# The h product in 64x64 waves, a slot of two 64x64 runs and two full-array phases, and PSUM as one pair plus three rotating pairs

## The chip, the cores and the metric

The kernel runs on one core of a Trainium2 chip. The metric is device time in microseconds, the median over repeated runs of the whole kernel; a profile is one further execution, taken by the hardware profiler, and its times are microseconds from the start of its span. The engines are PE (TensorE, matrix products, with PEld for its weight loads), DVE (VectorE), ACT (ScalarE), POOL (GpSimd) and SP (SyncE, which issues transfers). Each engine works through its own instructions in order and waits on semaphores for the others. PE writes its results to PSUM, eight banks of 512 fp32 values per partition; ACT and DVE read them from there.

## The reference

Four batches of eight heads run a state recurrence over 768 tokens with head size 40; its output, 3072 tokens by 320, goes through a two-layer block with a softmax weighting and a layer norm:

```python
for t in range(S):                       # S = 768, state is (B, H, 40, 40)
    y[:, :, t] = einsum('bhd,bhde->bhe', r[t], state)
    Sa = einsum('bhde,bhe->bhd', state, a[t])
    state = state * w[t][:, :, None, :] - outer(Sa, b[t]) + outer(v[t], k[t])
x = y.transpose(0, 2, 1, 3).reshape(3072, 320)
h = x @ w_in                             # 3072 x 1024
e = exp(h - max(h)); solu = h * e / (sum(e) + 1e-9)
ln = (solu - mean(solu)) / sqrt(var(solu) + 1e-6) * g_ln
out = ln @ w_out                         # 3072 x 320
```

The two weights arrive as fp64 and are converted to fp32 on the chip from their bits.

## The kernel before

The recurrence is done in chunks of 64 tokens. An item `i` (there are `N` = 24) is one chunk of two batches: 2 x 64 tokens, eight heads each, in 128 partitions. Two sequences of items alternate (even and odd `i`), so the state that item `i` leaves is next used by item `i + 2`. A hand-written order fixes every engine's instructions (`manual_schedule`): the main loop runs over slots `i` = -1 to 27, and in each slot works on several items at different stages:

- item `j = i + 5`: `front` and `front_b` transpose the raw `a` and the scaled `b` on PE (tiles `pa`, `pb`); DVE multiplies `pa` by the decays `ex` into `aT` (L374), ACT copies `pb` to `bT` (L359). `norm` multiplies them (`pnt`), DVE masks the result to `nt` (L383), and it goes through DRAM to `invert`, a triangular inverse done in 30 steps on DVE (L436, L438), of which `some(n)` issues `n` at a time. `decay` and `decay_turned` prepare the decays of items `j + 2` and `j + 1`: a product `pcum`, two exponentials on ACT, a transpose `pei`, and an ACT copy to `ex` (L366).
- item `i + 2`: `attend_kv` and `attend_r` transpose k, v and r (`pk`, `pv`, `pr`) and ACT copies each (L359).
- item `i + 1`: `scores` (`ps`, masked twice by DVE), `couple` (`py`) and `close` (`pz`), which finish the inverse, `carried` and `driven` (`px`).
- item `i`: `solved` (`pu`), `stated` (transposes of the state, `pst`, copied by ACT to `s`), `answered` (`pl`), `read` in two parts (`pyo`), and `leave`, in which DVE forms the output rows and the new state and SP and POOL (`left`, one slot later) move the rows to `xT` by DMA.
- item `i - 3`: `hidden`, the product `h = xT . w_in` of 128 x 1024 with a contraction of 320 that is cut into parts 128, 128 and 64; then `highest` (DVE, L678), `exped` (ACT), `weighed` and `spreadof` (DVE), and `folded` (eight transposes `plnT` in two halves, each copied by ACT to `lnT`, L721).
- item `i - 4`: `output`, `po = lnT . w2`, 8 products of 128x128x320, scaled by ACT to `osb` (L735), which issues the DMA to the output itself.

PE's products come in two shapes of the array. The recurrence's products use it as four tiles of 64x64 (16 products of up to 104 columns each per step; `in_turn` deals them out so that four neighbours lie in four different tiles). The transposes, `pcum`, `po` and the parts 0 and 1 of `h` use it whole; part 2 of `h` uses two tiles of 64 rows by 128 columns, because its contraction is 64. `fence()` is a PE drain; it stands once in every slot, ahead of the second half of `read`.

PSUM is divided by tag: `banks` (two buffers of two banks, for the 64x64 products), `h` (one buffer of two banks) and `bank` (two buffers of one bank, for transposes, `pcum`, `po`, `pmean`). A tile is free for its tag's next user when all its readers are done.

The order of PE in a slot far from the ends is: `pu`, `ps`, `pst`, `pa`, h(0,1), `pb`, `pei`, h(1,1), `pcum`, first half of `po`, `py`, `pnt`, `pl`, second half of `po`, `pz`, first half of `pyo`, `px`, h part 2, drain, second half of `pyo`, `px`, `plnT`, h(0,0), `pk`, `pv`, h(1,0), `pr`. The h of one item spans two slots.

Of the kernel before, what the change touches and what calls it, by code (L numbers as in the profile page):

```python
# [17 lines left out]
P = 128  # L18
# [6 lines left out]
LAG = 1  # L25


THIN = (5, 15)
# [23 lines left out]
def kernel(  # L52
# [34 lines left out]
    ps1 = ctx.enter_context(tc.tile_pool(name="ps1", bufs=2, space=PSUM))  # L87
    ps2 = ctx.enter_context(tc.tile_pool(name="ps2", bufs=1, space=PSUM))
    ps3 = ctx.enter_context(tc.tile_pool(name="ps3", bufs=2, space=PSUM))
# [49 lines left out]
    def banks(name):  # L139
        return ps1.tile([P, 2, 512], FP32, tag="banks", name=name)  # L140

    def bank(name):
        return ps3.tile([P, 512], FP32, tag="bank", name=name)
# [76 lines left out]
    def turn_g():  # L220
        pg = bank("pg")
        nc.tensor.transpose(out=pg[:, 0:NF], in_=g_rows, identity=ident[0:NF, 0:NF])
        for x, y in zip(g_cols, (0, -20, -36)):
            nc.scalar.mul(out=x, in_=pg[:, 0:NF], mul=2.0 ** y)
# [6 lines left out]
    def mean_of(lo, hi, begun):  # L231
        t = bank("pmean")
        nc.tensor.matmul(t[:, 0:DM], lhsT=ident, rhs=begun, start=True, stop=False)
        mean_part(t, lo, hi, False)
        return mean_kept(t)
# [90 lines left out]
    def decay(i):  # L326
        if not ok(i):
            return
        d = st[i]
        if "lw" not in d:  # L330
            logged(i)
        t = (bank("pcum") if i > 5 else ps2.tile([P, DFF], FP32, tag="h", name="h"))[:, 0:DM]
        nc.tensor.matmul(t, lhsT=c_("cum"), rhs=d["lw"], start=True, stop=True)  # L333
        nc.scalar.activation(out=ei_t[0][:, :, 0:D], in_=heads(t), func=AF.Exp)
        inv = d["inv"] = two.tile([P, DM], FP32, tag="inv", name="inv", bufs=4)
        nc.scalar.activation(out=inv, in_=t, func=AF.Exp, scale=-1.0)
# [10 lines left out]
    def turned(name, x):  # L347
        t = bank("p" + name)
        for j in range(4):
            nc.tensor.transpose(out=t[0:W2, j * P:(j + 1) * P],  # L350
                                in_=x[:, 2 * j:2 * j + 2].rearrange("p a b -> p (a b)")[:, 0:W2], identity=ident)
        return t[0:W2].rearrange("p (j b t) -> p b j t", j=4, b=2)
# [9 lines left out]
    def decay_turned(i):  # L362
        if not ok(i):
            return
        ex = st[i]["ex"] = ex_t[i % (AHEAD + 2)]
        nc.scalar.copy(out=ex[0:W2, :, :, 1:], in_=turned("ei", ei_t[0]))  # L366

    def front(i):
        if not ok(i):
            return  # L370
        d = st[i]
        t = turned("a", d["raw_a"])
        aT = d["aT"] = tokens("aT", AHEAD)
        nc.vector.tensor_tensor(out=aT[0:W2], in0=t, in1=d["ex"][0:W2, :, :, 0:C], op=ALU.mult)  # L374

    def front_b(i):
        if not ok(i):
            return
        d = st[i]
        d["bT"] = kept("bT", turned("b", d["kb"][:, H:]))  # L380
# [13 lines left out]
    def norm(i):  # L394
        if not ok(i):
            return
        d = st[i]
        t = banks("pnt")
        for u in in_turn(lambda p, q, g, h: (h, p ^ h)):
            p, q, g, h = u  # L400
            j = 2 * q + g
            mm(t[half(p ^ h), h, j * C:j * C + C], keyed(d["bT"], u), keyed(d["aT"], u))
        nt = d["nt"] = tokens("nt", AHEAD)
        masked(nt, t[:, :, 0:256])
        n, at = divmod(i, GRP)
        if at == 0:
            blocks[n] = dram.tile([2 * GRP * H, C, C], FP32, tag="nt_dram", name="nt_dram")
        queue = nc.sync if i < 4 else nc.gpsimd
        queue.dma_start(out=blocks[n].rearrange("(a h x) s c -> a x s h c", a=GRP, x=2)[at].rearrange("x s h c -> (x s) h c"),  # L409
                          in_=nt.rearrange("p h j c -> p (h j) c"))  # L410
# [56 lines left out]
    def couple(i):  # L467
        if not ok(i):
            return
        d = st[i]  # L470
        t = banks("py")
        for u in in_turn(lambda p, q, g, h: (p ^ h, p)):
            p, q, g, h = u
            j = 2 * q + g
            x = half(p ^ h)
            mm(t[half(p), h, j * Q:j * Q + Q], d["nt"][x, h, j], d["tu"][x, 4 * h + j, 0:Q])
        nc.scalar.activation(out=wy[:, :, :, 0:Q], in_=t[:, :, 0:4 * Q].rearrange("p h (j c) -> p h j c", j=4),  # L477
                             func=AF.Copy, scale=c_("neg_hi"))

    def close(i):  # L480
        if not ok(i):
            return
        d = st[i]
        t = banks("pz")
        for u in in_turn(lambda p, q, g, h: (p, p ^ h)):
            p, q, g, h = u
            j = 2 * q + g
            mm(t[half(p ^ h), h, j * Q:j * Q + Q], wy[half(p), h, j], d["uh"][half(p), 2 * (4 * h + j) + (p ^ h)])
        nc.scalar.copy(out=d["tu"].rearrange("p (h j) c -> p h j c", h=2)[:, :, :, 2 * Q:],
                       in_=t[:, :, 0:4 * Q].rearrange("p h (j c) -> p h j c", j=4))  # L490


    def attend_kv(i):
        if not ok(i):
            return
        d = st[i]
        d["kT"] = kept("kT", turned("k", d["kb"]))
        d["vT"] = kept("vT", turned("v", v_t[0]))

    def attend_r(i):  # L500
        if not ok(i):
            return
        st[i]["rT"] = kept("rT", turned("r", r_t[0]), 2)

    def stated(i):
# [4 lines left out]
        if ci:  # L510
            t = bank("pst")
# [6 lines left out]
    def scores(i):  # L518
# [3 lines left out]
        t = banks("ps")  # L522
# [13 lines left out]
    def carried(i):  # L536
# [5 lines left out]
        d["px"] = banks("px")  # L542
# [21 lines left out]
    def solved(i):  # L564
# [3 lines left out]
        t = banks("pu")  # L568
# [14 lines left out]
    def answered(i):  # L583
# [3 lines left out]
        t = banks("pl")  # L587
# [6 lines left out]
    def read(i, own):  # L594
# [4 lines left out]
        if own:  # L599
            d["po"] = banks("pyo")  # L600
# [60 lines left out]
    def hidden(i, some):  # L661
# [4 lines left out]
        for kt, x in some:  # L666
            if (kt, x) == (NK - 1, 0):
                d["h"] = ps2.tile([P, DFF], FP32, tag="h", name="h")
            part = slice(0, P) if kt < 2 else half(x)
            mm(d["h"][:, 512 * x:512 * x + 512], d["xT"][part, kt], w_in[part, 2 * kt + (x if kt < 2 else 0)],  # L670
               start=kt == NK - 1, stop=kt == NK - 2)
# [39 lines left out]
    def folded(i):  # L711
# [3 lines left out]
        lnT = d["lnT"] = two.tile([P, NF, P], FP32, tag="lnT", name="lnT", bufs=1)  # L715
        for x in range(2):
            t = bank("plnT")
# [5 lines left out]
    def output(i, x):  # L723
# [4 lines left out]
        if x == 0:  # L728
            d["out"] = bank("po")
        for f in range(x * NF // 2, x * NF // 2 + NF // 2):  # L730
            nc.tensor.matmul(d["out"][:, 0:DM], lhsT=d["lnT"][:, f, :], rhs=w2[:, f, :], start=f == 0, stop=f == NF - 1)  # L731
        if x == 0:
            return
        osb = two.tile([P, DM], FP32, tag="osb", name="osb", bufs=1)
        nc.scalar.activation(out=osb, in_=d["out"][:, 0:DM], func=AF.Copy, scale=d["rs"])  # L735
# [28 lines left out]
    decay(0)  # L764
    logged(1)
    decay_turned(0)
    for i in range(4):
# [6 lines left out]
        front_b(i)  # L774
        decay(i + 1)
# [3 lines left out]
        norm(i)  # L779
        decay_turned(i + 1)  # L780
# [28 lines left out]
    scores(0)  # L809
    decay(5)  # L810
# [12 lines left out]
    for i in range(-1, N + 3 + LAG):  # L823
        j, m = i + AHEAD, i - LAG
        pieces = shares.get(i, (0, 5, 4, 4) if i % GRP else (3, 5, 4, 5))
# [8 lines left out]
        if i in THIN:  # L834
            stated(i)
            front(j)
        if i >= 0:
            scores(i + 1)
        if i >= 0:
            load_keys(j + 3, "w")  # L840
        load_keys(j + 2, "bak")

        if i not in THIN:
            stated(i)
            front(j)
        hidden(m - 2, ((0, 1),))
        if i == 3 + LAG:
            centred(mean)
        narrow(some_weights[1], pieces[1])
        front_b(j)  # L850
        if ok(j + 2):
            logged(j + 2)
        if i == 1 + LAG:
            first = ps2.tile([P, DFF], FP32, tag="h", name="mean")
            mean_part(first, 0, 2, True, False)
        decay_turned(j + 1)
        hidden(m - 2, ((1, 1),))
        flip(i + 1)
        highest(m - 2)
        scaled(j + 1)  # L860
        left(i - 1)
        if i == 1 + LAG:
            mean_part(first, 2, 3, False)
            mean = mean_kept(first)
        decay(j + 2)
        output(m - 3, 0)

        some(pieces[2])
        if i == 2 + LAG:
            mean = mean_of(3, 6, mean)  # L870
        couple(i + 1)
        exped(m - 2)
        norm(j)
        answered(i)
        weighed(m - 2)
        spreadof(m - 2)
        if ok(j) and j % GRP == GRP - 1:
            begin_inverse(j // GRP)
        if i == 0:
            turn_g()  # L880
        output(m - 3, 1)

        close(i + 1)
        read(i, True)
        carried(i + 1)
        narrow(some_weights[2], pieces[3], ok(j) and j % GRP == GRP - 1)
        by_value(i + 2)
        if ok(m - 1):
            hidden(m - 1, ((2, 0), (2, 1)))
        fence()  # L890
        read(i, False)
        driven(i + 1)
        leave(i)
        begin_narrow(narrowed.get(i + 1, (0,))[0])
        folded(m - 2)
        hidden(m - 1, ((0, 0),))
        attend_kv(i + 2)
        hidden(m - 1, ((1, 0),))
        attend_r(i + 2)
        if i == 2 + LAG:  # L900
# [31 lines left out]
```

## Time and profile before

| | |
|---|---|
| median of 3 runs | 621.01 us (619.56 to 622.48) |
| span of the profiled execution | 616.2 us |
| granted TensorE clock, mean over the span | 0.928 |
| PE records in the trace | 11453 |
| DVE: the 30-step inverse, L436 and L438 | 99.2 + 102.1 us |
| HBM | 40.10 MB read, 13.37 MB written |

The profiled execution is one more run of the same kernel; its span is 4.8 us under the median. The profile's page gives busy time by engine, the span in 40 slices, the chain of work that ended last, and groups of instructions with their mean duration and the idle time ahead of them. The trace behind it can also be asked for a timeline, for waits by who ended them, and for windows, the busy time of every engine in a stretch. On PE a product of fp32 leaves two records and a transpose one; the ends of PE's records are modelled, so what a group costs is read from start to start. A PE record of `64*64` names rows and columns of the array that it uses.

The slices of the page (15.4 us each) show PE at five to six tenths in the first six, eight in the next three and nine from the tenth to the last but one; the granted clock is 0.5 to 0.8 in most of the first nine and printed as 9, which is 0.9 or more, in the rest up to the last. A slot begins with `pu`: its first records start at 65.8 us for item 0, at 161.3 us for item 4, at 443.5 us for item 17 and at 561.6 us for item 23, the last. From item 17 on a slot has less in it, since `front`, `norm` and the decays run out of items.

### The profile page before, as it was taken

The page shows a single profiled execution, that of the slowest core. Times are in us where ns is not written, and L with a number is a line of the kernel's source. Part 1 is how long each engine was busy: PE and PEld are TensorE (multiplying, and loading weights), DVE is VectorE, ACT ScalarE, POOL GpSimd, SP SyncE. Part 2 cuts the span into 40 slices and gives each one's busy share as a digit, 9 for nine tenths or more (in the row PEclk, how much of TensorE's full clock was granted, in tenths as well). Part 3 has the DMA queues.
Part 4 walks back from the last instruction along what each step waited for, and adds up shares of the span by engine and source line. Part 5 has one row for each costly group of instructions (what it writes and reads, how often), then busy time and mean ns, then how long its engine had stood idle before and what let it go on. Part 6 is the DMA issues. An engine that isn't in the chain of part 4 may idle for free.

```text
span 616.2 us, 26656 instructions
## 1 busy us (share of the span) xinstructions
PE 552.0 (90%) x11453; PEld 401.9 (65%) x11453; DVE 449.0 (73%) x1262; ACT 265.8 (43%) x548; POOL 258.0 (42%) x424
## 2 busy tenths in 40 slices
PE   5555668889999999999999999999999999999994
PEld 3333457666676777777777777777777676676652
DVE  4797986988968869869868868788697588443431
ACT  3433444654543544454444445444433343342221
POOL 3463264283453472473365355444624631322200
PEclk9665765789999999999999999999999999999998
DMA  7986887476455455564564474564532622310100
GB/s 164 159 156 121 183 157 129 98 156 104 76 106 104 90 115 99 93 122 95 100 123 91 95 126 98 112 113 82 110 56 53 118 49 43 65 35 26 28 19 21
DMA packets 213901, 59.93 MB, mean 97 GB/s; under 512 B 199120, under 2 KB 208952, under 8 KB 213784
## 3 DMA queue, kind: packets, MB, share of 16 engines
q1 hardware_dynamic: 195512, 33.78, 32.8%
q0 software_dynamic: 11568, 19.78, 14.0%
q10 hardware_dynamic: 6704, 4.67, 2.7%
q8 instruction: 90, 1.47, 1.0%
q14 instruction: 27, 0.22, 0.1%
HBM read 40.10 MB, written 13.37 MB: 87 GB/s over the span
## 4 chain that ended last, share of the span: by engine, by line
PE 74%; DVE 17%; ACT 3%; issue 3%; DMA 1%; ACTq 1%; DVEq 0%; SPq 0%
PE po L731 16%; PE h L265 16%; PE pyo L265 8%; DVE uu L438 5%; DVE prod L436 5%; PE pu L265 4%; PE plnT L720 4%; PE ps L265 4%; PE px L265 3%; PE py L265 2%; PE pl L265 2%; PE pz L265 2%; PE pr L350 2%; PE pst L513 2%; PE pcum L333 1%
## 5 line engine op out<-in xcount | busy, mean ns | idle before, releaser
L265 PE MATMUL h<-w_in,xT 128*128 128x512 f32 (+1 forms) x288 | 123.7, 614 | 0.0
L731 PE MATMUL po<-w,lnT 128*128 128x320 f32 x384 | 112.7, 438 | 0.5 <-ACT lnT L721 0.5
L438 DVE TENSOR_TENSOR uu<-uu,prod 128x30 f32<-128x30 f32 (+4 forms) x360 | 102.1, 284 | 12.4
L436 DVE TENSOR_TENSOR prod<-blk,uu 128x30 f32<-128x30 f32 (+4 forms) x360 | 99.2, 276 | 9.6
L731 PEld LDWEIGHTS po<-w,lnT 128*128 128x128 f32 x384 | 71.0, 190 | 32.6 <-issue 4.1
L409 POOL DMA_DIRECT2D nt_dram<-nt x20 | 18.8, 938 | 120.8 <-DVE nt L383 99.8
L709 POOL TENSOR_TENSOR rs<-c,mhalf 128x1 f32<-128x1 f32 x24 | 13.5, 561 | 112.3 <-DVE c L708 103.4
L383 DVE TENSOR_TENSOR psi<-ps,cst 128x512 f32<-128x512 f32 x24 | 16.6, 690 | 59.5 <-PE ps L265 59.5
L658 POOL DMA_DIRECT2D xT<-x x96 | 48.9, 514 | 0.4 <-DMA blk<-nt_dram 0.3
L265 PEld LDWEIGHTS h<-w_in,xT 128*128 128x128 f32 (+1 forms) x288 | 37.6, 190 | 9.4 <-issue 8.1
L678 DVE TENSOR_REDUCE nmax<-h 128x1 f32<-128x1024 f32 x24 | 28.6, 1193 | 18.6 <-PE h L265 18.6
L420 POOL DMA_DIRECT2D blk<-nt_dram x46 | 36.9, 808 | 11.8 <-issue 8.4
L265 PE MATMUL pyo<-lv,kb 64*64 64x104 f32 x768 | 38.3, 269 | 2.2
L265 PEld LDWEIGHTS pyo<-lv,kb 64*64 64x64 f32 x768 | 24.1, 142 | 21.2 <-issue 21.1
L265 PE MATMUL pyo<-lu,kb 64*64 64x104 f32 x768 | 37.4, 262 | 0.1
L646 POOL TENSOR_TENSOR st<-tot,ex 104x160 f32<-104x160 f32 x44 | 21.7, 511 | 36.4 <-DVE tot L642 32.4
L562 ACT COPY x<-px 128x320 f32<-128x320 f32 x24 | 10.2, 426 | 56.3 <-PE px L265 56.1
L477 ACT ACTIVATE wy<-py,cst 128x256 f32<-128x256 f32 x24 | 11.4, 474 | 53.2 <-PE py L265 53.2
L288 POOL DMA_DIRECT2D raw_r<-in_r_dram x48 | 33.9, 709 | 0.0
L735 ACT ACTIVATE osb<-po,rs 128x320 f32<-128x320 f32 x24 | 12.7, 527 | 48.5 <-PE po L731 32.8
L686 ACT ACTIVATE e<-h,nmax 128x1024 f32<-128x1024 f32 x24 | 26.6, 1108 | 14.3 <-DVE nmax L678 14.3
L692 DVE TENSOR_TENSOR e<-h,e 128x1024 f32<-128x1024 f32 x24 | 29.2, 1217 | 4.7 <-ACT e L686 4.7
(131 smaller groups left out, 1169.1 us busy)
## 6 DMA issues: line engine op xcount, KB each, us to landing
blk<-nt_dram POOLq DMA_DIRECT2D x46, 128.0 KB, 4.7
nt_dram<-nt POOLq DMA_DIRECT2D x20, 256.0 KB, 3.7
raw_w<-in_w_dram SPq DMA_DIRECT2D x48, 80.0 KB
a<-in_a_dram SPq DMA_DIRECT2D x48, 80.0 KB
raw_r<-in_r_dram POOLq DMA_DIRECT2D x48, 80.0 KB, 3.6
lv<-in_v_dram SPq DMA_DIRECT2D x48, 80.0 KB
out_dram<-osb ACTq DMA_DIRECT2D x24, 160.0 KB
raw_b<-in_b_dram SPq DMA_DIRECT2D x44, 80.0 KB
```

Source lines behind the costliest of these rows:

```text
L265: nc.tensor.matmul(o, lhsT=lhsT, rhs=rhs, start=start, stop=stop, skip_group_check=True)
L288: queue.dma_start(out=x[half(p), :, 0:D], in_=ap[2 * bp + p, :, ci * C:(ci + 1) * C, :].rearrange("h t d -> t h d"))
L420: queue.dma_start(out=nb[home:home + Q], in_=blocks[n][:, Q * e:Q * e + Q, Q * e:Q * e + Q])
L436: nc.vector.tensor_tensor(out=t, in0=nb[:, j:j + 1, j + 1:Q].to_broadcast([P, n_c, m]), in1=u[:, 0:n_c, j:j + 1].to_broadcast([P, n_c, m]) ...
L438: nc.vector.tensor_tensor(out=u[:, 0:n_c, j + 1:Q], in0=u[:, 0:n_c, j + 1:Q], in1=t, op=ALU.subtract)
L646: nc.gpsimd.tensor_tensor(out=to3(old), in0=to3(tot[0:W2]), in1=ex[:, :, 2 * q:2 * q + 2, C:].to_broadcast([W2, 2, 2, D]), op=ALU.mult)
L658: nc.gpsimd.dma_start(out=xT[to:to + Q, 2], in_=x[at + P - 3 * D:at + D, 2])
L678: nc.vector.tensor_reduce(out=nmax, in_=d["h"], axis=AX.X, op=ALU.max, negate=True)
L686: nc.scalar.activation(out=e, in_=d["h"], func=AF.Exp, bias=d["nmax"], accum_out=d["esum"])
L692: nc.vector.tensor_tensor(out=d["e"], in0=d["h"], in1=d["e"], op=ALU.mult)
L720: nc.tensor.transpose(out=t[:, j * P:(j + 1) * P], in_=d["e"][:, f * P:(f + 1) * P], identity=ident)
L731: nc.tensor.matmul(d["out"][:, 0:DM], lhsT=d["lnT"][:, f, :], rhs=w2[:, f, :], start=f == 0, stop=f == NF - 1)
```

## The change

- **h.** Every part of h is done in waves of four 64x64 products of 512 columns: `hidden(i, ((kt, phase),))` issues, for both halves `y` of the contraction rows and both halves `col` of the 128 tokens, one product into bank `y ^ phase`. Part 2 (64 deep) needs one wave, since both row halves hold the same tokens against different columns of `w_in`; parts 0 and 1 need two each. All five waves of an item now stand in one slot.
- **Order.** The slot becomes two runs of 64x64 products and two full-array phases: `pu`, h(2,0), `ps`, h(0,0), `pl`, h(1,0); then `pab` (a and b), `pes` (decays and state), `pcum`; then `pnt`, first half of `pyo`, `px`, h(0,1), `py`, h(1,1), `pz`, second half of `pyo`, `px`; then all of `po`, `pkv`, `pr`, `plnT`. `LAG` goes from 1 to 3 with the loop's stage offsets taken out, so h still serves item `i - 3` and `po` item `i - 4`; the loop has the same slots.
- **Fence.** The drain stays only where `i >= N` and once at `i == N - 1`.
- **PSUM.** One pool of pairs of banks, each tag with one buffer: `h`, and `pair0` to `pair2`, taken as `(k + i) % 3`. Transposes that had a bank each now share a pair: `a` and `b` in `pab`, the decays and the state in `pes`, `k` and `v` in `pkv`, the two halves of `plnT` in one pair. `pcum`, `po`, `pr` and `pmean` use half a pair.
- The steps of the inverse are dealt out as (0, 3, 5, 5) and (3, 3, 5, 6) for (0, 5, 4, 4) and (3, 5, 4, 5): 30 in two slots as before. `output` is one piece. On ACT, `by_value` stands ahead of `couple` and `close`, `osb` and its DMA ahead of the copies of k and v, and those ahead of `lnT`. On DVE, the mask `lu` stands ahead of `aT`, and `highest` behind `norm`.

```diff
-    ps1 = ctx.enter_context(tc.tile_pool(name="ps1", bufs=2, space=PSUM))
-    ps2 = ctx.enter_context(tc.tile_pool(name="ps2", bufs=1, space=PSUM))
-    ps3 = ctx.enter_context(tc.tile_pool(name="ps3", bufs=2, space=PSUM))
+    psum = ctx.enter_context(tc.tile_pool(name="psum", bufs=1, space=PSUM))
...
+    turn = [0]
+    def pair(k, name):
+        return psum.tile([P, 2, 512], FP32, tag="h" if k == "h" else f"pair{(k + turn[0]) % 3}", name=name)
...
-    def front(i):
+    def front(i, k=0):
         d = st[i]
-        t = turned("a", d["raw_a"])
+        t = pair(k, "pab")
+        at = turned(t[:, 0], d["raw_a"])
         aT = d["aT"] = tokens("aT", AHEAD)
-        nc.vector.tensor_tensor(out=aT[0:W2], in0=t, in1=d["ex"][0:W2, :, :, 0:C], op=ALU.mult)
-
-    def front_b(i):
-        d["bT"] = kept("bT", turned("b", d["kb"][:, H:]))
+        nc.vector.tensor_tensor(out=aT[0:W2], in0=at, in1=d["ex"][0:W2, :, :, 0:C], op=ALU.mult)
+        d["bT"] = kept("bT", turned(t[:, 1], d["kb"][:, H:]))
...
-        d["kT"] = kept("kT", turned("k", d["kb"]))
-        d["vT"] = kept("vT", turned("v", v_t[0]))
+        t = pair(1, "pkv")
+        d["kT"] = kept("kT", turned(t[:, 0], d["kb"]))
+        d["vT"] = kept("vT", turned(t[:, 1], v_t[0]))
...
-        for kt, x in some:
-            if (kt, x) == (NK - 1, 0):
-                d["h"] = ps2.tile([P, DFF], FP32, tag="h", name="h")
-            part = slice(0, P) if kt < 2 else half(x)
-            mm(d["h"][:, 512 * x:512 * x + 512], d["xT"][part, kt], w_in[part, 2 * kt + (x if kt < 2 else 0)],
-               start=kt == NK - 1, stop=kt == NK - 2)
+        for kt, phase in some:
+            if (kt, phase) == (NK - 1, 0):
+                d["banks"] = pair("h", "h")
+                d["h"] = d["banks"].rearrange("p x n -> p (x n)")
+            for y in range(2):
+                for col in range(2):
+                    x = y ^ phase
+                    mm(d["banks"][half(col), x], d["xT"][half(y), kt, half(col)],
+                       w_in[half(y), 2 * kt + (x if kt < 2 else 0)], start=kt == NK - 1, stop=(kt, phase) == (1, 1))
...
+        both = pair(0, "plnT")
         for x in range(2):
-            t = bank("plnT")
+            t = both[:, x]
             for j in range(NF // 2):
                 f = x * (NF // 2) + j
                 nc.tensor.transpose(out=t[:, j * P:(j + 1) * P], in_=d["e"][:, f * P:(f + 1) * P], identity=ident)
             nc.scalar.copy(out=lnT[:, x * (NF // 2):(x + 1) * (NF // 2)].rearrange("p f t -> p (f t)"), in_=t)
```

The new slot, without the parts that only the first slots have:

```python
        solved(i)
        hidden(m, ((2, 0),))
        scores(i + 1); load_keys(j + 3, "w"); load_keys(j + 2, "bak")
        hidden(m, ((0, 0),))
        answered(i)
        hidden(m, ((1, 0),))
        front(j)
        narrow(some_weights[1], pieces[1]); logged(j + 2)
        t = pair(2, "pes")
        decay_turned(j + 1, t[:, 0])
        stated(i, t[:, 1])
        flip(i + 1); scaled(j + 1); left(i - 1); decay(j + 2)
        norm(j)
        some(pieces[2])
        read(i, True); carried(i + 1)
        hidden(m, ((0, 1),))
        by_value(i + 2); couple(i + 1)
        hidden(m, ((1, 1),))
        highest(m); close(i + 1)
        read(i, False); driven(i + 1)
        exped(m); leave(i); weighed(m); spreadof(m)
        narrow(some_weights[2], pieces[3], ok(j) and j % GRP == GRP - 1)
        output(m - 1)
        attend_kv(i + 2); attend_r(i + 2)
        folded(m)
```

## The prediction

> **What bounds the kernel now.** First the windows view, cut where items 0, 4, 17 and 23 begin (columns: length; then busy us of PE, PEld, DVE, ACT and POOL, each with its instructions; granted clock; DMA share; GB/s):
>
> ```profile
> 65.80:161.30 95.50, 74.35 (x1733) 58.52 (x1733) 83.45 (x233) 48.46 (x102) 46.27 (x71) 0.78 0.68 131
> 161.30:443.50 282.20, 279.42 (x6267) 205.40 (x6266) 222.05 (x636) 130.35 (x273) 136.59 (x223) 1.00 0.55 104
> 443.50:561.60 118.10, 115.68 (x2689) 83.97 (x2688) 77.92 (x222) 47.02 (x95) 41.76 (x75) 1.00 0.31 61
> ```
>
> Thirteen slots fill 282.2 us, 21.7 us each, with PE busy for 99%; DVE is busy for 79%. Before 161.3 us PE has gaps and a lower clock. So the change is priced on PE's timeline, from start to start, in one full slot (302.33 to 323.86 us, 21.53 us, and its neighbours):
>
> ```profile
> 305.66 0.36 PE L265 MATMUL pyo<-lv,kb 64*64 64x104 f32 x8
> 305.85 0.36 PE L265 MATMUL pyo<-lu,kb 64*64 64x104 f32 x8
> ...
> 307.03 1.13 PE L265 MATMUL h<-w_in,xT 64*128 64x512 f32 x4
> 308.25 0.41 PE L265 MATMUL pyo<-lv,kb 64*64 64x104 f32 x8
> ...
> 315.08 0.65 PE L265 MATMUL ps<-rT,vT 40*64 40x64 f32 x32
> 315.66 0.64 PE L513 MATMUL pst<-cst,st 128*104 128x128 f32 x4
> 316.14 0.60 PE L350 MATMUL pa<-cst,a 128*104 128x128 f32 x4
> 316.57 1.02 PE L265 MATMUL h<-w_in,xT 128*128 128x512 f32 x2
> 317.43 0.60 PE L350 MATMUL pb<-cst,kb 128*104 128x128 f32 x4
> 317.87 0.60 PE L350 MATMUL pei<-cst,ei 128*104 128x128 f32 x4
> ...
> 322.46 0.67 PE L265 MATMUL pnt<-aT,bT 40*64 40x64 f32 x32
> 323.23 0.69 PE L265 MATMUL pl<-rT,nuT 40*64 40x64 f32 x32
> 323.86 2.42 PE L731 MATMUL po<-w,lnT 128*128 128x320 f32 x8
> ```
>
> Groups follow without gaps: four transposes take 0.44, a 128x512 product 0.86, a step of sixteen small products 0.49. ACT's timeline of the same slot gives what a reader of PSUM costs:
>
> ```profile
> 318.07 0.59 ACT L359 COPY bT<-pb 104x512 f32<-104x512 f32 x1 [1.15 <-PE pb L350]
> 318.55 0.47 ACT L324 ACTIVATE lw<-raw_w 128x320 f32<-128x320 f32 x1
> 318.92 0.58 ACT L366 COPY ex<-pei 104x512 f32<-104x512 f32 x1
> ...
> 326.31 0.53 ACT L735 ACTIVATE osb<-po,rs 128x320 f32<-128x320 f32 x1 [2.04 <-PE po L731]
> 326.87 0.52 ACTq L736 DMA_DIRECT2D out_dram<-osb  x1
> 327.44 0.37 ACT L489 COPY tu<-pz 128x256 f32<-128x256 f32 x1 [0.59 <-PE pz L265]
> ```
>
> A copy starts 0.20 after its transposes end (317.87 to 318.07), lasts 0.58, and lets PE go 0.06 after its end (`wy` ends at 323.17, `pl` starts at 323.23).
>
> **The change part by part, for a full slot.**
>
> *h.* Before: four products of 0.86 and part 2 at 1.22 (307.03 to 308.25). After: five waves of four 64x64 products. No row shows a wave of 512 columns. The nearest is `pyo`: four products of 104 columns, eight records, in 0.18 us, 1.7 ns a column for both passes, like the full product's 0.86/512. So a wave is taken at 0.86 and the streaming stays at 4.3 us; if only two of the four ran at once it would be 1.72, 4.3 us more a slot; no row allows less than 0.86.
>
> *Changes of array shape.* To the full array costs 0.13 with transposes (`ps` 0.58 instead of 0.49; `pst` 0.48 instead of 0.44) and 0.17 to 0.23 with `po`; back costs 0.09 to 0.12 (`pr` 0.53 instead of 0.44). Around part 2 lie 0.11 ahead, 0.36 in it (1.22 less 0.86, the drain among it) and 0.045 behind. `pl` also waits 0.28 (0.77 from `pnt` to `pl` instead of 0.49) for `wy`. Before: 0.13 + 0.23 + 0.13, three times 0.10, 0.515 and 0.28: 1.59. After, two changes each way: 0.13 + 0.17 + 0.10 + 0.11 = 0.51. Saved 1.08; the slot would be 20.45.
>
> *Shared pairs.* This decides. The built instruction list of the changed kernel gives the second half of each shared pair a wait that the list of before doesn't have: `b`'s first transpose in `pab` waits for the count that DVE reaches with `aT`, the state's in `pes` for ACT's `ex`, v's in `pkv` for ACT's `kT`, and the fifth of `plnT` for ACT's first `lnT`. Each waits until the *first* half has been read, though it writes the other bank. Before, these were separate tiles in two buffers, and `plnT`'s eight transposes are one row without a wait. PE runs in order, so all products queue behind, and nothing else is there to hide it:
> - `pab`: 0.20 + 0.68 (`aT`, L374, mean 683 ns) + 0.06 = 0.94.
> - `pes`: ACT takes `bT`, `lw`, `ex` in this order, the first 0.20 after `pab` ends: 0.20 + 0.48 + 0.37 + 0.58 + 0.06 = 1.69, less the 0.44 of the decays' transposes: 1.25.
> - `pkv`: ACT first takes `osb` and its DMA issue, 1.13 (326.31 to 327.44): 0.20 + 1.13 + 0.59 + 0.06 = 1.98, less 0.44: 1.54.
> - `plnT`: `vT`, `rT`, then `lnT`: 0.20 + 0.49 + 0.50 + 0.59 + 0.06 = 1.84, less 0.88 for `pr` and the first half: 0.96.
>
> Together 4.7; weight loads that wait too are no longer ahead (0.04 to 0.10 at a change of shape): 0.2 more, 4.9. The least is four bare copies, 4 x 0.84 = 3.4. Net 4.9 - 1.1 = +3.8 a slot (2.3 to 3.8).
>
> *What stays covered:* `s` to `pyo` 0.85, under `pcum` and `pnt` (1.13); `wy` to `pz` 0.73, under an h wave (0.86); `tu` to `po` 0.63, under `pyo` and `px` (1.2); h's max, exponential and product (1.19 + 1.11 + 1.22 and some 0.5 of handing on) under 6 us up to `plnT`. Were one uncovered, PE would lose the difference, 0.3 or so. The dropped drain is in the 0.36. The inverse ends later in its slot, so its two DMAs on SP, the next `bring` and the loads behind it start later; SP then has some 25 us for what took it some 15, and `xT` is needed three slots on: nothing.
>
> *Sum over the stages.* Up to 65.8 us: six or seven such waits at about 1, partly beside waits for loads: +7 (0 to 12). Items 0 to 3: four `pab`, two `pes`, four `pkv`, one `plnT`, 13; ACT's conversions of the weights (0.62 + 0.62 + 0.64 a part) now stand ahead of `kT`: 18 (5 to 30). Items 4 to 16: 13 x 3.8 = 49. Items 17 to 22: 3.8, then without `pes` 2.5, three times 1.5 without `pab`, then 0: 11. Rest: four `plnT` waits, less the part-2 changes: +4 (0 to 8). Total 89.
>
> *Clock.* The gaps may also cost clock:
>
> ```profile
> 15.30:18.70 3.40, 1.59 (x38) 1.00 0.96 153
> 18.70:22.10 3.40, 1.66 (x8) 0.51 0.83 156
> ...
> 155.30:158.70 3.40, 1.93 (x11) 1.00 0.03 11
> ```
>
> These are windows of PE alone (length; PE busy; clock; DMA). After 3.4 us with PE busy for 1.59 the clock halves; after 1.93 it stays. The granted clock changes in steps of 3.4 us. The emptiest 3.4 us of the new slot hold 1.2 us of streaming in `pab`/`pes` and 1.3 in `pkv`/`plnT`, about 1.5 as this view counts: under the limit where a step falls right on them. A step at half clock loses at least 1.7. Taken: one slot in four, 24 x 0.25 x 1.7 = +10 (0 to 60). The Trainium skill ("TensorE: Matmul & The Clock Gate", section "Why this matters for your kernels") warns only of PE gaps over about 3 us. By it this term is 0, as no new gap passes 1.6; but the stretch at 15.3 us has no gap over 1.7 either, and its row decides.
>
> 616.2 + 89 + 10 = 715 for the profiled span; the median of the runs lies 4.8 above the profile: **720 us**.
>
> **The rivals.**
> - *The clock falls in most slots.* 24 slots at 1.7 to 3.4 instead of the +10: 751 to 792, say 765. For: the window of 1.59. Against: a slot has ten dense microseconds that win the clock back, and the steps drift against it. 20%.
> - *The waits cost half* (readers quicker in their turn, the early stages hiding theirs): 44 instead of 89, no clock loss: 665. Against: the four sums hold nothing but durations. 13%.
> - *Faster: the waits are met.* If the first halves had been read whenever the second is due, the 1.08 saved stands alone: 18 slots x 1.08 = 19, 602 us. It decides once the four waits sum to less than 1.08, 0.27 each; one copy with its handing on takes 0.84. 4%.
> - *The waves stream two at a time:* 24 x 4.3 = 103 more, 823. Against: the `pyo` rows. 4%.
> - *No change to speak of:* saving and waits cancel within 3 us. 1%.
>
> The forecast itself (695 to 745) has 58%.
>
> **How the numbers follow.** The range of 8 in 10 is 680 to 775: it takes in most of the clock's case and part of the half-priced waits. The bound of what a measurement tells from no change is 0.5%, 3 us. Faster 4%, same 1%, slower 95%.
>
> **What would show it.** In the changed profile: `pab`, `pes`, `pkv` and `plnT` among PE's idle times, released by DVE `aT` and ACT `ex`, `kT` and `lnT`, at 0.9, 1.3, 1.5 and 1.0 each; slots of some 25.3 us; four records of 512 columns per 0.43; no gap at `pl`. Half clock after 160 us shows the clock's case. Waves at 1.7, or PE running through the pairs without gaps, would make the forecast wrong.

## The result and the profile after

The changed kernel takes 749.2 us (median of 4 runs, 746.9 to 753.1) against 620.3 us for the kernel before in the same session (median of 4, 618.9 to 622.5): 1.208 times as long, 95% interval 1.203 to 1.214. Its profiled execution has a span of 748.5 us, 132.3 more than the 616.2 of before. Executions more than 1.5% above the fastest of their kernel are left out of all ratios below, but not of the medians; this touches E2 and E3 alone, and the profiles of both are of such executions.

First the windows view, cut at the starts of the same items as before (columns: length; busy us of PE, PEld, DVE, ACT, POOL; granted clock; DMA share; GB/s):

```profile
75.10:196.10 121.00, 77.78 (x1752) 60.12 (x1751) 79.95 (x233) 48.97 (x102) 50.23 (x76) 0.71 0.58 105
196.10:535.10 339.00, 283.52 (x6634) 204.59 (x6633) 226.49 (x630) 130.45 (x273) 131.33 (x214) 0.98 0.43 82
535.10:683.60 148.50, 123.01 (x2857) 88.19 (x2856) 79.08 (x222) 46.64 (x94) 42.42 (x76) 0.94 0.26 52
```

In items 4 to 16 PE is busy for 283.5 us, 4 more than before, but the stretch is 339.0 long instead of 282.2: PE stands still for 55 us where it stood still for 3. Against before the stages grew by 9.3 us (up to item 0), 25.5 (items 0 to 3), 56.8 (4 to 16), 30.4 (17 to 22) and 10.3 (the rest).

What PE waited for in items 4 to 16, from its waits (engine, tile, line, releaser: us in total, times, longest):

```profile
PE pkv L346 <- ACT kT L355: 18.7, 13, 1.6
PE pes L505 <- ACT ex L362: 14.1, 13, 1.1
PE pab L346 <- DVE aT L371: 10.5, 12, 0.9
PE plnT L716 <- ACT lnT L717: 10.1, 13, 0.8
```

All four are second halves of a pair, released by the reader of the first half, once in almost every slot. They sum to 53.4 of the 55 us in which PE stands still. The kernel before shows no wait of PE over 0.2 us there. One clean slot on PE's timeline, 404.85 to 430.11 us (start, length, operation, in brackets the idle time before it):

```profile
405.80 1.08 PE L262 MATMUL h<-w_in,xT 64*64 64x512 f32 x8
406.69 0.66 PE L262 MATMUL ps<-aT,kT 40*64 40x64 f32 x32
...
409.94 0.65 PE L346 MATMUL pab<-cst,a 128*104 128x128 f32 x4
411.46 0.62 PE L346 MATMUL pab<-cst,kb 128*104 128x128 f32 x4 [0.87 <-DVE aT L371]
411.91 0.60 PE L346 MATMUL pes<-cst,ei 128*104 128x128 f32 x4
413.60 0.65 PE L505 MATMUL pes<-cst,st 128*104 128x128 f32 x4 [1.08 <-ACT ex L362]
...
425.21 0.60 PE L346 MATMUL pkv<-cst,kb 128*104 128x128 f32 x4
427.23 0.65 PE L346 MATMUL pkv<-cst,v 128*104 128x128 f32 x4 [1.42 <-ACT kT L355]
...
428.15 0.60 PE L716 MATMUL plnT<-cst,e 128*128 128x128 f32 x4
429.53 0.66 PE L716 MATMUL plnT<-cst,e 128*128 128x128 f32 x4 [0.78 <-ACT lnT L717]
```

A wave of four 64x64 products with 512 columns (eight records) takes 0.89 from start to start. From a first half's start to the second's, less 0.44 for the four transposes, the pairs cost 1.08, 1.25, 1.58 and 0.94: 4.85 us of a slot of 25.26.

The clock is the rest of the middle. Windows of PE alone (length, PE busy, clock, DMA share, GB/s) around three of its falls:

```profile
229.00:232.40 3.40, 1.44 (x12) 1.00 0.44 75
232.40:235.80 3.40, 3.40 (x65) 0.50 0.48 79
...
307.50:310.90 3.40, 1.44 (x12) 1.00 0.59 100
310.90:314.30 3.40, 3.40 (x70) 0.51 0.00 0
...
488.40:491.80 3.40, 1.11 (x9) 1.00 0.45 78
491.80:495.20 3.40, 3.40 (x58) 0.51 0.63 101
```

Each of these half-clock steps follows a window in which the emptied slot left PE busy for under 1.5 of 3.4 us; so do the other falls between items 4 and 22 but one, where PE was busy for 1.54. Between items 4 and 22 the changed kernel has 33 us at half clock in this execution; before had none.

### The profile page after: what moved, and what is told of

It reads as the page before. It is cut to its first block, busy times and chain, and to the rows that moved or that the text cites. A ratio compares the mean times of both kernels' runs of the same rounds, so it can differ in the third digit from the quotient of the medians.

```text
span 748.5 us, 27974 instructions
## 1 busy us (share of the span) xinstructions
PE 572.0 (76%) x12125; PEld 406.2 (54%) x12125; DVE 453.3 (61%) x1262; ACT 267.1 (36%) x548; POOL 258.8 (35%) x424
## 4 chain that ended last, share of the span: by engine, by line
PE 57%; ACT 12%; DVE 11%; DMA 7%; issue 7%; SPq 4%; ACTq 1%; POOL 1%; POOLq 0%; DVEq 0%
PE h L262 13%; PE po L726 9%; PE pyo L262 7%; PE pab L346 3%; PE pu L262 3%; DMA uu_dram<-uu 3%; SPq L285 3%; PE px L262 2%; PE pcum L330 2%; PE ps L262 2%; DVE uu L430 2%; PE pnt L262 2%; PE plnT L716 2%; PE pes L505 2%; DVE prod L428 2%
## 5 line engine op out<-in xcount | busy, mean ns | idle before, releaser
L262 PE MATMUL h<-w_in,xT 64*64 64x512 f32 x960 | 129.8, 603 | 0.3
L428 DVE TENSOR_TENSOR prod<-blk,uu 128x30 f32<-128x30 f32 (+4 forms) x360 | 94.9, 264 | 10.3 <-DMA blk<-nt_dram 0.4
L638 POOL TENSOR_TENSOR st<-tot,ex 104x160 f32<-104x160 f32 x44 | 22.2, 520 | 119.3 <-DVE tot L634 112.2
L704 POOL TENSOR_TENSOR rs<-c,mhalf 128x1 f32<-128x1 f32 x24 | 13.4, 560 | 129.6 <-DVE c L703 129.6
L346 PE MATMUL pkv<-cst,v 128*104 128x128 f32 x96 | 17.7, 314 | 51.4 <-ACT kT L355 51.4
L355 ACT COPY bT<-pab 104x512 f32<-104x512 f32 x24 | 14.0, 585 | 116.9 <-PE pab L346 116.9
L375 DVE TENSOR_TENSOR nt<-pnt,cst 128x512 f32<-128x512 f32 x24 | 16.5, 688 | 55.1 <-PE pnt L262 55.0
L716 PE MATMUL plnT<-cst,e 128*128 128x128 f32 x192 | 31.4, 287 | 22.1 <-ACT lnT L717 18.8
L346 PE MATMUL pab<-cst,kb 128*104 128x128 f32 x96 | 17.7, 314 | 35.9 <-DVE aT L371 34.6
L346 PEld LDWEIGHTS pkv<-cst,v 128*104 128x104 f32 x96 | 10.9, 144 | 57.9 <-ACT kT L355 57.9
L330 PE MATMUL pcum<-lw,cst 128*128 128x320 f32 x48 | 24.8, 609 | 19.0 <-ACT lw L321 19.0
L716 PEld LDWEIGHTS plnT<-cst,e 128*128 128x128 f32 x192 | 21.7, 144 | 30.5 <-ACT lnT L717 24.6
```

What stands on the lines that cost most here:

```text
L262: nc.tensor.matmul(o, lhsT=lhsT, rhs=rhs, start=start, stop=stop, skip_group_check=True)
L346: nc.tensor.transpose(out=t[0:W2, j * P:(j + 1) * P], in_=x[:, 2 * j:2 * j + 2].rearrange("p a b -> p (a b)")[:, 0:W2], identity=ident)
L375: nc.vector.tensor_tensor(out=dst, in0=t.rearrange("p b (j c) -> p b j c", j=4), in1=tri.unsqueeze(1).unsqueeze(1).to_broadcast([P, 2, 4, ...
L428: nc.vector.tensor_tensor(out=t, in0=nb[:, j:j + 1, j + 1:Q].to_broadcast([P, n_c, m]), in1=u[:, 0:n_c, j:j + 1].to_broadcast([P, n_c, m]) ...
L716: nc.tensor.transpose(out=t[:, j * P:(j + 1) * P], in_=d["e"][:, f * P:(f + 1) * P], identity=ident)
```

## The experiments

E1 to E12 each differ from the changed kernel, or from one another, by a few lines. The ratio is to the kernel before on the same chip. "Even" and "odd" are the median lengths of even and odd slots in items 4 to 16 of one profile.

| | kernel | median us | ratio, 95% interval | even, odd slot |
|---|---|---|---|---|
| | changed | 749.2 | 1.208, 1.203 to 1.214 | 25.3, 25.5 |
| E1 | both halves first | 705.6 | 1.141, 1.134 to 1.148 | 21.8, 27.0 |
| E2 | the same in `pkv`, `plnT` only | 718.5 | 1.157, 1.150 to 1.164 | 23.3, 26.7 |
| E3 | the same in `pab`, `pes` only | 721.9 | 1.156, 1.146 to 1.167 | 24.1, 26.0 |
| E4 | changed, `by_value` back | 742.2 | 1.198, 1.191 to 1.206 | 25.3, 25.8 |
| E5 | E1, v's load ahead of `bring` | 676.8 | 1.090, 1.081 to 1.099 | 22.2, 23.6 |
| E6 | E5, flip and last steps moved | 726.8 | 1.173, 1.165 to 1.181 | 24.4, 27.7 |
| E7 | E6, `lw` ahead of `bT` | 719.0 | 1.160, 1.151 to 1.169 | 23.8, 27.9 |
| E8 | changed, with the moves of E5 and E6 | 765.8 | 1.235, 1.228 to 1.243 | 27.2, 27.3 |
| E9 | E5, `lw` ahead of `bT` | 674.1 | 1.087, 1.078 to 1.095 | 21.9, 23.5 |
| E10 | E9, last steps moved | 661.4 | 1.068, 1.059 to 1.076 | 21.4, 24.1 |
| E11 | E9, h in full-array products | 699.5 | 1.127, 1.118 to 1.135 | 22.8, 26.1 |
| E12 | changed, v's load ahead of `bring` | 749.2 | 1.211, 1.203 to 1.218 | 25.3, 26.2 |

**E1: are the waits the loss?** Both halves are transposed before either is read:

```diff
-        at = turned(t[:, 0], d["raw_a"])
+        at, bt = turned(t[:, 0], d["raw_a"]), turned(t[:, 1], d["kb"][:, H:])
...
-        d["bT"] = kept("bT", turned(t[:, 1], d["kb"][:, H:]))
+        d["bT"] = kept("bT", bt)
```

and likewise k and v in `pkv`, decays and state in `pes`, the eight transposes in `plnT`.

> In all four shared pairs both halves are transposed before either is read; nothing else is moved, and all is computed. Theory (the waits of the second halves are the loss): the 1.08, 1.25, 1.59 and 1.09 us at pab, pes, pkv and plnT go, a clean slot falls from 25.3 to 20.2-20.7 us, the nine steps at half clock after 198 us go with the gaps, and the time falls by 18 x 5.0 = 90 in the slots with all four waits, some 35 in the other stages and up to 15 of clock: 595 to 630 us, below or at the kernel before. Rival (h in waves, the new order or the rotation of three pairs is the loss): the time stays above 690 and the slot above 24 us. Rival (half of it is the clock, and the clock falls for another reason than the gaps): the waits go, but steps at half clock remain and the time lies at 640 to 680.

Measured: 705.6 us. The four waits are gone from PE's list, and even slots fall by 3.5 us, to 21.8. Odd slots do not fall; they rise from 25.5 to 27.0. So 44 us go, not 140: the time lies where the first rival had it, above 690, while the even slots fell by most of what the theory said. PE's timeline of an odd slot that starts at 303.86 shows what holds it:

```profile
314.67 1.07 PE L262 MATMUL h<-w_in,xT 64*64 64x512 f32 x8
316.90 0.67 PE L262 MATMUL py<-tu,nt 64*64 64x32 f32 x32 [1.16 <-DVE nt L375]
317.39 1.07 PE L262 MATMUL h<-w_in,xT 64*64 64x512 f32 x8
...
320.39 1.08 PE L262 MATMUL pz<-uh,wy 64*64 64x32 f32 x32 [1.93 <-ACT wy L469]
```

SyncE's and ScalarE's timelines of that slot carry it back:

```profile
304.68 1.30 SPq L436 DMA_DIRECT2D uu_dram<-uu  x2
313.25 1.03 SPq L449 DMA_DIRECT2D tu<-uu_dram  x2
314.33 0.98 SPq L451 DMA_DIRECT2D uh<-uu_dram  x2
315.42 1.75 SPq L285 DMA_DIRECT2D lv<-in_v_dram  x2
```

```profile
319.14 0.46 ACT L316 COPY v<-lv 128x320 f32<-128x320 f32 x1 [5.74 <-DMA lv<-in_v_dram]
319.51 0.45 ACT L316 COPY r<-raw_r 128x320 f32<-128x320 f32 x1
319.87 0.47 ACT L469 ACTIVATE wy<-py,cst 128x256 f32<-128x256 f32 x1
```

The inverse's last step ends after the slot has begun; its write is issued at 304.68; the fetch of `tu` waits on SyncE until 313.25; v's load stands behind the fetches at 315.42; ScalarE, which meets `by_value` ahead of `wy`, waits 5.74 us for it; `wy` releases `pz` at 320.39. PE has so little to do meanwhile that the clock falls (half clock from 319.8 to 326.6). This is a second bound, once every two slots, that lay beside the four waits: in items 4 to 16 PE waits at `pz` for `wy` for 13.1 us, where the changed kernel has no such wait.

**E2 and E3: one phase at a time.**

> Only pkv and plnT have both halves transposed before the copies; pab and pes stay as they are; all is computed. Theory: each wait has its own price and they add: 1.59 + 1.09 = 2.7 us off a full slot (25.3 to 22.6), 18 x 2.7 = 48 plus some 15 in the early and late stages plus half of the clock's loss: 670 to 695 us. Rival (the next wait takes over, so that one pair's fix is worth little without the other's): the idle time at pab and pes grows, and the time stays above 715.

> Only pab and pes have both halves transposed before the readers; pkv and plnT stay as they are; all is computed. Theory: 1.08 + 1.25 = 2.3 us off a full slot (25.3 to 23.0), 17 x 2.3 = 40 plus some 10 in the early stages plus part of the clock's loss: 685 to 710 us, and the reductions of this kernel and of the one with pkv and plnT alone add up to that of both within 10 us. Rival (waits take over from one another): the idle time at pkv grows and the time stays above 725.

Both ended near 720 us, E2 above its range and E3 a little above. The gains, 0.051 and 0.052 of the time of before, add to 0.104, where both edits together bring 0.067: some 23 us less than the sum, with about 10 either way by the intervals. The waits that each edit left in place hardly changed, where the rivals had them grow: in items 4 to 16 those at `pab` and `pes` are 12.3 and 13.4 us in E2, after 10.5 and 14.1, and that at `pkv` is 18.7 in E3, as before. The shortest even slots add (25.25 to 22.86 and to 24.07, together 3.6; E1's shortest is 21.69, 3.6). The odd slots gain nothing from either edit (medians of 26.7 and 26.0, against 25.5 in the changed kernel), and `pz` waits for `wy` there already, 8.2 us in E2 and 4.2 in E3. So it is in the odd slots that each edit's gain is cut off.

**E5: v's load ahead of the fetches**, on top of E1:

```diff
-        if i >= 1:
-            bring(i + 1)
         if i >= 0:
             load_values(i + 2)
+        if i >= 1:
+            bring(i + 1)
```

> The kernel with both halves first (705.6 us), and on SyncE's queue the load of v for item i+2 stands ahead of the two fetches of the inverse (bring) instead of behind them; all is computed. Theory (a second bound: in each odd slot the fetch waits for the inverse's write to DRAM, some 8 us, v's load waits behind it in the same queue, ScalarE's copy of v waits for the load, wy behind that copy and PE at pz): pz's 21.8 us of idle time go, the odd slots fall from 27-28 to 24-25.5 us, part of the half-clock steps go with them, 660 to 688 us. Rival (the fetch itself holds the slot: the flip of the inverse waits for it, nt behind the flip on VectorE, py behind nt): the odd slots stay above 26.5 us and PE's idle time moves from pz to py; 695 to 705 us. Rival (the long odd slots are the clock's own steps): no change.

Measured: 676.8 us, 29 less than E1 with clearly separate intervals; PE's idle time at `pz` falls from 21.8 to 2.4 us, odd slots from 27.0 to 23.6, and the time at half clock between items 4 and 22 from 45 to 16 us. The order of two transfers on one queue was the main part of the second bound.

**E4 and E12: what that is worth under the waits.** E12 is the same edit on the changed kernel; E4 moves ScalarE's copies of v and r behind `close` instead.

> The changed kernel with ScalarE's copies of v and r moved back behind pz (as in the kernel before they stood behind py and pz); all four shared waits stay. Theory (in items 17 to 22 the copy of v waits for its load, wy waits behind it and PE waits at pz): the 4.4 us of PE idle at pz<-wy in the late stage go, the alternation of the late slots (28.2, 21.3, 26.4 us) is smaller by some 2.5 us in the long ones, and the time falls by 4 to 8 us: 741 to 746 us. Rival (the long late slots are steps at half clock and nothing else): pz's waits go but the time stays within 3 us of the changed kernel.

> The changed kernel with its four waits, and only v's load ahead of bring on SyncE's queue; all is computed. Theory (under the waits the inverse's chain is covered in the full slots and costs only where slots are shorter): items 4 to 16 stay at 25.3 us a slot, the late stage falls by 5 to 9 us, 736 to 746 us; the same edit that is worth 29 us without the waits is worth 4 to 12 with them. Rival (both add): it falls by 25 us or more, below 726 us.

In both profiles `pz`'s idle time falls from 6.8 to 2.4 us and items 17 to 22 get shorter, 140.5 us in E4 and 143.4 in E12 against 148.5. Items 4 to 16 hardly do: 335.6 and 339.0 against 339.0. The medians are 742.2 and 749.2; both intervals overlap the changed kernel's, so the few microseconds of the late stage are not settled by the time. E4's median lies in its forecast of 741 to 746; E12's forecast of 736 to 746 was missed. What it does show: an edit worth 29 us without the waits is worth nothing measurable with them.

**E6, E7, E8: the whole chain moved, wrongly.** Beside E5's edit the slot's last steps of the inverse (with the early slots' weight conversions, all issued by one call of `narrow`) went in front of `read(i, False)`, and `flip(i + 1)`, VectorE's transpose of the fetched part of the inverse within `tu`, behind `norm(j)` and the steps after it:

```diff
-        flip(i + 1)
         scaled(j + 1)
...
         some(pieces[2])
+        flip(i + 1)
```

> The kernel with both halves first, v's load ahead of bring, the flip of the inverse behind VectorE's nt and the steps after it, and the slot's last steps of the inverse (with the early items' weight conversions) in front of read(i, False), where they end about 7 us before the slot does; all is computed. Theory (the inverse's chain from its last step over DRAM to pz is the second bound): odd slots fall to the even ones' 21.7 us, half-clock steps after 198 us go, items 4 to 16 take 13 x 21.7 = 282 instead of 316 us, and the time is 635 to 665 us. Rival (the three rotating pairs or VectorE hold the odd slots): they stay above 25 us and the time above 685 us.

> The changed kernel with its four waits left as they are, and only the inverse's chain moved ahead (v's load before bring, the flip behind nt, the last steps earlier); all is computed. Theory (the waits alone hold the clean slots at 25.3 us and the chain fits under them, so that it costs only where slots are shorter): items 4 to 16 stay at 25.3 us a slot plus clock steps, the late stage falls by 5 to 10 us and the early one by up to 8: 728 to 745 us. Rival (the chain and the waits lie one behind the other): it falls as much as with both halves first, by 40 us or more, below 710 us.

> As the kernel with the chain moved ahead, and ScalarE's logarithm lw stands ahead of the copy of bT, which in the built program waits for VectorE's aT although it reads the other half of the pair; all is computed. Theory (pcum waits 0.6 to 1.1 us a slot for lw behind that copy): 0.6 to 1.0 off every slot, 21.7 to 20.8-21.1, 18 x 0.7 = 13 us less than the kernel without this edit: 620 to 652 us. Rival (the next wait takes over, pnt for bT or pyo for s): within 4 us of the kernel without it.

All three forecasts were missed: E6 is 50 us slower than E5, E8 17 slower than the changed kernel. The waits of E6 in items 4 to 16 name the cause:

```profile
PE py L262 <- DVE tu L457: 32.7, 13, 4.5
```

The flip now queues behind five pairs of inverse operations on VectorE: in the slot at 363.7 `nt` starts at 376.40 and the flip only at 379.63, and `py` waits 2.5 us a slot for it, even and odd. E10 below differs from E7 in the place of the flip alone; there this wait is gone in these items (31.7 us in E7), and the time is 661.4 instead of 719.0 us. So the flip's new place alone cost 58 us. These three do not test the theory they were meant for; they price that edit. E7's 8 us against E6 are short of the 13 forecast, and the intervals overlap slightly.

**E9, E10: the edits one by one.** In E9 `logged(j + 2)`, ScalarE's logarithm `lw`, stands ahead of `front(j)`; in E10 `narrow(some_weights[2], pieces[3])` also moves to just behind `close(i + 1)`, and the flip stays where it was.

> The kernel with both halves first and v's load ahead of bring (676.8 us), and ScalarE's logarithm lw ahead of the copy of bT, which in the built program waits for VectorE's aT of the other half; all is computed. Theory (pcum waits 0.6 to 1.1 us a slot for lw behind that copy): the 12 or so us of that wait outside the early items go, 0.6 to 0.8 a slot: 657 to 670 us, even slots at 21.0 us. Rival (the next wait takes over: pyo for s, pnt for bT): within 4 us of 676.8.

> As the kernel with v's load and lw ahead, and the last steps of the inverse in a slot stand on VectorE in front of x, tot and the h product instead of behind them (some 7 us earlier); the flip stays where the changed kernel has it. All is computed. Theory (what is left of the second bound is the inverse's end: write, fetch, flip, nt, py): py's idle time on nt and tu (some 10 us) goes, odd slots come within 0.7 us of the even ones, 640 to 658 us. Rival (the steps then delay x, tot and the product on VectorE, which PE waits for at plnT or pes): equal or slower than the kernel without it.

E9's time came out as the rival had it, though another wait took over than those it named: `pcum`'s waits for `lw` outside the early items are gone (41.9 us in all to 26.0, all of that in four waits before item 0), yet the time moved by 2.7 us, inside the intervals. `py` waits longer for `nt` instead (7.6 to 15.4 us).

E10 brought 13 us, 3 short of its forecast, and not where the theory had it. Items 0 to 3 fell from 111.3 to 105.0 us: some weight conversions now stand on ScalarE ahead of the copy `x` instead of the copies of k and v, so that `pu` waits there for `vT` 4.0 us instead of 15.1 and `pkv` for `x` 8.3 instead of 2.2; `pmean`'s wait for `lnT` falls from 8.0 to 1.2 as well. Items 17 to 22 fell from 130.9 to 123.7, nearly all of it PE's busy time (119.2 to 112.3): 10 us at half clock in E9, none in E10. Items 4 to 16 gained 2 us. VectorE's timeline of an odd slot that starts at 424.9 shows the other end of the inverse's loop:

```profile
433.09 0.47 DVE L422 TENSOR_SCALAR uu<-blk 64x512 f32<-64x512 f32 x1 [1.28 <-DMA blk<-nt_dram]
433.63 0.07 DVE L423 MEMSET uu<- 64x16 f32 x1
436.06 0.19 DVE L428 TENSOR_TENSOR prod<-blk,uu 128x30 f32<-128x30 f32 x1 [2.35 <-DMA blk<-nt_dram]
...
437.34 0.44 DVE L457 STREAM_TRANSPOSE tu<-tu 128x256 f32<-128x256 f32 x1
437.70 0.65 DVE L375 TENSOR_TENSOR nt<-pnt,cst 128x512 f32<-128x512 f32 x1
```

With PE faster, the next inverse's first steps come up before their blocks are back from DRAM; the flip and `nt` queue behind them, and `py` waits. Giving odd slots their first steps later was not tried.

**E11: are the waves a loss?** E9 with h in the products of before, (2,0) and (2,1) with a drain at the first place, one 128x128 product at each other.

> As the kernel with v's load and lw ahead, but h is computed as in the kernel before, in products of 128x128 with 512 columns and the two 64x128 ones with a drain behind them, at the places where the waves stand; all is computed. Theory (the waves stream at the full array's rate, and what they save are changes of shape and the drain): four more visits to the full array at 0.23 to 0.35 each plus 0.1 to 0.4 for the drain, 1.0 to 1.8 us a slot, 20 to 38 us slower than the kernel with waves: 683 to 702 us. Rival (the waves cost more than they save): equal or faster than the kernel with waves.

Measured: 699.5 us, 25 slower than with waves, inside the forecast. Even slots are 0.9 us longer by the median, 1.5 by the shortest (22.64 against 21.15). PE's timeline of one slot has the changes of shape:

```profile
405.51 1.13 PE L262 MATMUL h<-w_in,xT 64*128 64x512 f32 x4
406.74 0.69 PE L262 MATMUL ps<-aT,kT 40*64 40x64 f32 x32
407.25 0.65 PE L262 MATMUL ps<-rT,vT 40*64 40x64 f32 x32
407.83 1.12 PE L262 MATMUL h<-w_in,xT 128*128 128x512 f32 x2
408.88 0.69 PE L262 MATMUL pl<-rT,nuT 40*64 40x64 f32 x32
409.51 1.13 PE L262 MATMUL h<-w_in,xT 128*128 128x512 f32 x2
```

From the second `ps` run to h there are 0.58 us instead of the 0.46 of a step, and from h to `pl` 1.05 instead of 0.86; part 2 with its drain takes 1.23, where the wave takes 0.89. At these places the waves are a gain. Not all of the 25 us is their price: in items 4 to 16 E11's profile has 24 us at half clock and E9's 7, which is up to 8 us of it.

No version beat the kernel before; the best, E10, is 6.8% slower.

## Why the prediction was right, point by point

*The size and the mechanism.* Forecast 720 (680 to 775), measured 749.2. This is above the 695 to 745 of the forecast itself and 2 us under the rival in which the clock falls in most slots, but that rival's cause is not there: 33 us at half clock between items 4 and 22 are some nine or ten steps in nineteen slots. No term was too large by more than 2, so none made up for another; the range held by the room it left above. The four waits came at the pairs named, with the releasers named: 1.08, 1.25, 1.58 and 0.94 us, 4.85 together, for forecasts of 0.94, 1.25, 1.54 and 0.96 (4.9 with the weight loads). Clean slots are 25.3 us, as forecast; without the four waits the one shown is 20.41, where the prediction had 20.45. `pl` no longer waits, and four 64x64 products of 512 columns stream in 0.86 to 0.89, not 1.7. Items 4 to 16: 13 times the 3.65 us between clean slots is 47 (forecast 49), four half-clock steps at up to 1.7 are 7 of the remaining 9, and PE's other waits in that stretch are 2.1.

*The terms that were too small.* Items 0 to 3 grew by 25.5, not 18: the second half of `pkv` alone waits 24.0 us in four slots, up to 8.2 at once, because ScalarE's conversions stand ahead of `kT`; the term had the mechanism and not its size. It counted ScalarE's three operations a part, 1.88 us; in three of the four slots the first operation of a part also waits 2.5 to 3.5 us for VectorE's `scale`. The wait and, for the longest one, the end of ScalarE's part:

```profile
PE pkv L346 <- ACT kT L355: 24.0, 4, 8.2
```

```profile
153.07 0.56 ACT L184 ACTIVATE scale<-scale,top 128x320 int32<-128x320 int32 x1 [2.75 <-DVE scale L182]
153.66 0.56 ACT L185 ACTIVATE scale<-scale,top 128x320 int32<-128x320 int32 x1
154.13 0.64 ACT L191 ACTIVATE w<-w,g,g 128x320 f32<-128x320 int32 x1
154.68 0.56 ACT L355 COPY kT<-pkv 104x512 f32<-104x512 f32 x1
```

Items 17 to 22 grew by 30.4, not 11. In that stretch PE stands still for 25.5 us, 23.1 more than before: 14.2 at the shared pairs (`pkv` 7.1, `plnT` 4.6, `pab` 1.8, `pes` 0.7), 4.4 at `pz`, 2.7 at `pyo` for `s`, 4.2 in smaller ones. The other 7.3 are longer busy time; 17 us run at half clock, which cost up to 8.5. The term counted the pairs alone. The first and last stretches grew by 9.3 and 10.3, for 7 and 4. The clock as a whole has 33 us at half rate between items 4 and 22, up to 16 lost, for a forecast of 10.

*The step that failed.* "The inverse ends later in its slot, so its two DMAs on SP, the next `bring` and the loads behind it start later; [...]: nothing." It named the right queue and weighed only `xT` at its far end. E1 and E5 show v's load behind the fetch on SyncE, and E1's trace the rest: `by_value` behind the load and ahead of `wy` on ScalarE, `pz` behind `wy`. In the changed kernel itself this shows, from item 4 on, only in two late waits of up to 2.5 us, since the four waits keep the full slots long enough. But for that reason the rival forecasts built on the waits (602 if they were met, 665 at half price) were worth less than they looked: with the waits removed altogether the kernel is still at 705.6. "The slot would be 20.45" holds as what PE's terms come to beside the waits (20.41), but for no whole slot: the shortest even slots are 21.7 in E1, with `pcum` waiting 0.57 for `lw`, and `pes` and `pu` some 0.4 together, and 21.15 at the shortest in E9.

*The shape changes.* Forecast 1.08 us a slot saved, for the changes of shape, the drain and the wait at `pl` together. The changed kernel's clean slot without its four waits is 1.12 shorter than the 21.53 of before, which bears the sum out. E11 puts the full-array products at the places of the waves, not at those of the kernel before, and loses 0.9 to 1.5 us a slot: of the changes of shape by themselves the sign and the order of size are shown, the figure is not.

*The clock rule.* "After 3.4 us with PE busy for 1.59 the clock halves" was one row. Six of the seven falls of the changed kernel between items 4 and 22 come after less than 1.50, but 1.59 is no boundary: the last section has the rows on both sides.

*What stays open.* E10 is still 40 us longer than before by the profiles: 4.1 up to item 0, 9.5 in items 0 to 3, 13.7 in 4 to 16, 5.6 in 17 to 22, and 7.2 in the rest. The waits for the inverse's blocks lie in the middle part (`py` waits 9.8 us there for `nt`); the 7.2 at the end come with h three slots behind instead of spread over two, which is argued and not tested.

## What to carry to other kernels

When two results share one tile, issue all writes of the tile before its first reader: the order of issue alone was worth 44 us here. Before pricing a wait at its length, ask what else would be due when it is gone, following each in-order queue to its last customer: here a DMA queue in which a load that waits for nothing stood behind a fetch that waits for everything. And an edit's worth depends on what binds beside it: the same swap of two transfers was worth 29 us and nothing.

## What the runs showed of the hardware that was not expected

The granted clock followed the sum of PE's busy time more closely than its gaps. It changed at whole multiples of one step: the half-clock rows of the changed kernel begin at 232.4, 310.9 and 491.8 us, which is 23 and then 53 steps of 3.413 us apart. Of the steps at full clock in all fourteen profiles, 118 had PE busy for less than 1.50 us by this view, and half clock followed each of them; it followed none with more than 2.12; between these it followed 45 and not the other 189. The longest single gap tells them apart less well: half clock followed a step whose longest gap was 0.79 us (E1, the step from 16.0, PE busy for 1.95), and did not follow one with a gap of 1.91 (E12, the step from 737.1, PE busy for 1.50). Between 0.78 and 1.92 lie 82 steps with a fall behind them and 340 without. The longest single gap in the step from 229.0 to 232.4 us was 1.08 us, ahead of `pes`. The Trainium skill ("TensorE: Matmul & The Clock Gate", section "Why this matters for your kernels") names PE-idle gaps over some 3 us as what costs clock; here steps with gaps a third of that long did.

Two readers of different halves of one PSUM tile, on two engines, did not overlap in E1: ScalarE's copy of `bT` started 0.04 us after VectorE's `aT` had ended (310.79 after 310.06 + 0.69), though the transposes of its own half had started at 309.43 and take 0.44, and were done 0.9 us before. In the built program the copy waits for VectorE's count; so this is a wait that the tracking of the tile adds, and no run shows whether the memory itself would have allowed both.
